# A spectral layer and two MLPs on one core: the first half's instructions issued from one written list of 1092 pieces

## The chip, the cores and the metric

One Trainium2 chip, one of its cores. The metric is the device time of one execution, in microseconds (us). The engines are PE (TensorE, matrix products; PEld is its weight load), DVE (VectorE), ACT (ScalarE), POOL (GpSimd) and SP (SyncE, which issues the DMAs here). Each engine runs its own instructions strictly in their order and waits at the head of its queue until what that instruction needs is there.

## The reference

```python
X = np.fft.fft(x, axis=1)            # x: 2 x 3008 x 256
X = np.fft.fft(X, axis=2)
x = X.real.reshape(6016, 256)
h = x @ w_in                         # 256 x 2048
x = np.maximum(h, 0.0) ** 2 @ w_out  # 2048 x 256
h = x @ w2_in
return h * (1.0 / (1.0 + np.exp(-1.702 * h))) @ w2_out
```

The weights come as float64 words, which the kernel itself turns into a high and a low float32r part.

## The kernel before

The work has three stages on one core.

**Folds and transforms.** The input is loaded in six pieces (`load_x`, L117; three per batch). A *fold* (`fold`, L275) adds and subtracts mirrored positions on DVE and POOL, and then multiplies with a table of cosines and sines on PE (L317). `even_k` (L373) and `odd_k` (L405) finish the transform for the four blocks of frequencies of a batch (L361 on PE) and split each block into a high and a low part (`split_eo`, L364). There are eight blocks, four per batch.

**The first MLP** is 128 *steps*, one for each pair of a block and one of 16 groups of 128 hidden features (`turns`, L445). A step has a *front* (`front1`, L451): six matmuls into two PSUM banks (tile `psa`; the pool has two places). Then DVE makes `p` and two `h` from these banks (L805, L807, L808), ACT takes relu and square (L814, L815; for the steps in `SV`, DVE does both in one instruction, L812), ACT casts to the high part `gh` (L817), and the low part `gl = h - gh` is subtracted on POOL or, for the ten steps in `VSTEPS`, on DVE (both print as L78). Four steps later (`LAG`) the *back* (`back`, L467) adds 12 matmuls (L477) into two PSUM tiles `psb`. Below, F8 is the front of step 8 and B8 its back. `h` and `gh` rotate through five places, `gl` through four.

The weights of both MLPs are widened in the background of the steps: `narrow` (L164) turns the words into float32 by six instructions on ACT and DVE (L171 to L187), `widen` (L194) makes the two parts. Eight such groups of the first MLP are loaded and widened while its steps already run, and so are four of the second MLP's.

**The second MLP** (L872, L856 and what lies between) is written by hand in an explicit order, `manual_schedule`, and begins where the first MLP's last front ends.

**What sets the order before.** `start` (L517) emits the first three folds and the first transforms; then the loop over the steps emits one front, one back, the DVE and ACT work of the step, and calls `background` (L567), which takes a few pieces from the running jobs by the rates and due times of the table `PLAN` (L32). From step 18 (`THROTTLE`) a job's pieces are held behind the step's own work. The tile framework's scheduler then orders the emitted instructions of each engine.

## Time and profile before

| | |
|---|---|
| three runs | 974.51, 975.67 (median), 976.25 us |
| the profiled execution | 974.99 us, span 973.2 us |
| mean granted TensorE clock | 0.998 |
| DMA | 53.58 MB, mean 55 GB/s |

The span is the time from the first to the last instruction. A busy PE in the profile is not PE at its peak: the ends of pipelined matmuls are modelled, so two matmuls that follow each other at 0.17 us each show 0.33 us. Prices below are therefore taken from start to start.

### The profile page before, as it was taken

What the parts mean: (1) busy time and instruction counts of PE and PEld (TensorE: products, weight loads), DVE (VectorE), ACT (ScalarE), POOL (GpSimd) and SP (SyncE); (2) the same over time, 40 slices, a digit from 0 to 9 for tenths busy, and PEclk for the clock granted to TensorE, in tenths of its full rate; (3) what the DMA queues carried; (4) which work ended last, traced back from release to release, by engine and by line L of the source; (5) the groups of instructions that cost most, each with busy time, mean ns of one, the idle gap of its engine ahead of it and who ended that gap; (6) DMA issues with size and microseconds to landing.
All of it is one profiled execution on the core that took longest, in us unless ns stands there. A gap on an engine that the chain in (4) does not pass through costs nothing.

```text
span 973.2 us, 12586 instructions
## 1 busy us (share of the span) xinstructions
PE 954.7 (98%) x4872; PEld 852.9 (88%) x4872; DVE 699.6 (72%) x870; ACT 599.6 (62%) x700; POOL 329.3 (34%) x203
## 2 busy tenths in 40 slices
...
GB/s 303 208 148 64 76 133 93 137 35 57 9 67 44 33 1 47 67 6 33 51 112 44 1 87 0 1 65 22 1 44 43 1 1 82 1 1 10 34 1 39
DMA packets 21899, 53.58 MB, mean 55 GB/s; under 512 B 3280, under 2 KB 15184, under 8 KB 19152
## 3 DMA queue, kind: packets, MB, share of 16 engines
...
q8 instruction: 38, 0.62, 0.3%
q14 instruction: 21, 0.17, 0.1%
...
## 4 chain that ended last, share of the span: by engine, by line
PE 76%; DVE 5%; ACT 3%; issue 1%; DVEq 0%; ACTq 0%
PE psb L872 26%; PE psc L856 23%; PE psb L477 17%; PE psa L462 3%; PE psa L464 3%; PE psa L463 3%; PE psa L361 1%; ACT h L815 1%; ACT h L814 1%; ACT gh L817 1%; DVE h L807 1%; DVE p L805 0%; DVE h L808 0%; PE psa L317 0%; DVE ue L185 0%
## 5 line engine op out<-in xcount | busy, mean ns | idle before, releaser
L78 POOL TENSOR_TENSOR gl<-h,gh 128x752 fp32r<-128x752 f32 (+1 forms) x118 | 223.2, 1897 | 152.5 <-ACT gh L817 108.6
L477 PE MATMUL psb<-gh,w 128*128 128x376 f32 (+1 forms) x1024 | 237.3, 335 | 0.2 <-ACT h L814 0.2
L477 PEld LDWEIGHTS psb<-gh,w 128*128 128x128 f32 x1024 | 182.6, 188 | 0.7 <-ACT h L814 0.4
L872 PE MATMUL psb<-gh,w 128*128 128x512 f32 (+1 forms) x576 | 163.7, 386 | 0.0
L936 DVE TENSOR_TENSOR g<-u,psc 128x1024 f32<-128x1024 f32 (+1 forms) x48 | 57.6, 1201 | 115.4 <-PE psc L856 115.4
L814 ACT ACTIVATE h<-h 128x752 f32<-128x752 f32 (+1 forms) x114 | 94.8, 833 | 58.1 <-DVE h L808 48.0
L477 PE MATMUL psb<-gl,w 128*128 128x376 f32 (+1 forms) x512 | 130.1, 335 | 0.0
L938 ACT ACTIVATE g<-g 128x1536 f32<-128x1536 f32 (+1 forms) x48 | 70.4, 1467 | 95.1 <-DVE g L936 95.1
L872 PEld LDWEIGHTS psb<-gh,w 128*128 128x128 f32 x576 | 108.1, 188 | 20.6
L817 ACT CAST gh<-h 128x752 fp32r<-128x752 f32 (+1 forms) x128 | 105.1, 822 | 31.8 <-DVE h L812 28.5
L78 DVE TENSOR_TENSOR gl<-g,gh 128x2048 fp32r<-128x2048 f32 (+1 forms) x48 | 109.5, 2282 | 1.2 <-ACT gh L913 1.2
L638 POOL TENSOR_TENSOR ue<-raw 128x512 f32<-128x512 f32 (+1 forms) x10 | 21.5, 2165 | 255.0 <-DMA raw<-ydram 173.6
L805 DVE SCALAR_TENSOR_TENSOR p<-n,w1n_t,psa 128x376 f32<-128x376 f32 (+1 forms) x128 | 76.5, 600 | 43.3 <-PE psa L464 43.1
L815 ACT ACTIVATE h<-h 128x752 f32<-128x752 f32 (+1 forms) x114 | 95.2, 836 | 3.1
L462 PE MATMUL psa<-eo,w 128*128 128x376 f32 (+1 forms) x256 | 88.1, 345 | 5.0 <-DVE h L808 2.7
L477 PEld LDWEIGHTS psb<-gl,w 128*128 128x128 f32 x512 | 92.6, 188 | 0.0
L913 ACT CAST gh<-g 128x2048 fp32r<-128x2048 f32 (+1 forms) x48 | 90.3, 1881 | 0.1
L872 PE MATMUL psb<-gl,w 128*128 128x512 f32 (+1 forms) x288 | 87.7, 386 | 0.0
L463 PE MATMUL psa<-eo,w 128*128 128x376 f32 (+1 forms) x256 | 85.8, 335 | 0.0
L464 PE MATMUL psa<-eo,w 128*128 128x376 f32 (+1 forms) x256 | 85.6, 334 | 0.0
L807 DVE TENSOR_TENSOR h<-p,psa 128x376 f32<-128x376 f32 (+1 forms) x128 | 69.7, 545 | 13.9 <-POOL gl L78 1.0
L935 ACT ACTIVATE g<-psc 128x512 f32<-128x512 f32 (+1 forms) x48 | 28.3, 590 | 76.0 <-PE psc L856 76.0
...
## 6 DMA issues: line engine op xcount, KB each, us to landing
...
xt<-in_x SPq DMA_DIRECT2D x5, 1024.0 KB, 7.0
...
raw<-in_w1i SPq DMA_DIRECT2D x4, 1024.0 KB, 4.9
raw<-in_w1o SPq DMA_DIRECT2D x4, 1024.0 KB, 5.8
raw<-in_w2i SPq DMA_DIRECT2D x4, 1024.0 KB, 4.9
raw<-in_w2o SPq DMA_DIRECT2D x4, 1024.0 KB, 4.9
```

Source lines behind the costliest of these rows:

```text
L78: eng.tensor_tensor(out=o, in0=a, in1=f32(b), op=ALU.subtract)
L462: T.matmul(o, lhsT=w[:, 0, fs], rhs=t[:, par, 0, 0:wd], start=True, stop=False)
L463: T.matmul(o, lhsT=w[:, 0, fs], rhs=t[:, par, 1, 0:wd], start=False, stop=False)
L464: T.matmul(o, lhsT=w[:, 1, fs], rhs=t[:, par, 0, 0:wd], start=False, stop=True)
L477: T.matmul(acc[j][ec][:, s, 0:wd], lhsT=w[:, hl, e0:e0 + P], rhs=(gh, gl)[gi][:, s, 0:wd], start=(first and hl == 0 and gi == 0), stop=(la ...
L807: V.tensor_tensor(out=h[:, 0, 0:wd], in0=p[:, 0:wd], in1=ps[:, 1, 0:wd], op=ALU.add)
L814: A.activation(out=hv, in_=hv, func=AF.Relu)
L815: A.activation(out=hv, in_=hv, func=AF.Square)
L817: last_a = A.copy(gh[:, :, 0:wd], hv)
L856: T.matmul(bank, lhsT=w[:, hl, slot * P:(slot + 1) * P], rhs=x[:, yl, 0:wd], start=(first and hl == 0 and yl == 0), stop=(hl == 1), skip_g ...
L872: T.matmul(o[:, s, 0:wd], lhsT=w[:, hl, e0:e0 + P], rhs=g[:, 2 * i + s, 0:wd], start=(f == 0 and hl == 0 and g is gh), stop=(f == 15 and h ...
L913: A.copy(gh, gs[u - 1])
```

## The change

Everything up to the last step of the first MLP is cut into 1092 named pieces, and a written list `ORDER` says in which order they are issued, under `manual_schedule`. `PLAN`, the rates and the background jobs are gone. The names: `f0D` loads input piece 0, `f0s0`, `f0a0`, `f0p`, `f0m`, `f0u` are its sums and differences, `f0E` and `f0O` its products on PE, `f0e0`, `f0o` the moves out of PSUM; `e00..` and `o0..` belong to the transforms of a batch (`E`, `N` products, `c`, `n` copies, `s`, `m` sums, `h`, `l` the two parts); `i0..` to `u3..` widen the first MLP's input and output weights, `j..` and `v..` the second's (`D` load, `A` `L` `C` `S` `O` `P` the six instructions of `narrow`, `H` and `l` the parts). Of step 8, `F8` is the front, `P8` the three DVE instructions, `R8` relu and square, `H8` the cast, `G8` the low part, `B8` the back.

With it some work changes its engine (`HOME`): 43 of the 128 subtractions `G` are on DVE, where ten were; 22 steps have relu and square on DVE, where 14 had; all subtractions of the first three folds are on DVE, where POOL had half or all of them; of the stores' copies six go from DVE to ACT and three from ACT to DVE. Some products of the start go to `psb` (`IN_B`). The two banks of a `psa` tile are now places of their own, and the turn in which `h`, `p` and the banks are taken is written out (`RINGS`). Fold 0 leaves out one sum (`u`) and has PE add instead: 12 products where there were 8, twice. Of the products with zeros that only keep PE at work (`keep_busy`) 26 stay of 48. From the second MLP on nothing changes.

```diff
-PLAN = {
-    "out0": (0, 12, 3), "even01": (0, 1, 4), "odd0": (1, 1, 48), "conv": (3, 1.2, 36),
-    "x3": (14, 1, 20), "x4": (33, 1, 34), "fold3": (31, 1.5, 40), "fold4": (38, 1.5, 46), "fold5": (45, 1.5, 52),
-    "cst": (30, 5, 45), "even10": (53, 1, 56), "even11": (52, 1, 58),
-    "cst3": (66, 4, 67), "odd1": (79, 1, 88), "w2a": (58, 1, 84), "w2b": (88, 1, 112), "y0": (111, 1, 128),
-}
...
-WARM = {0: 36, 2: 4, "first": 3, "second": 5}
-THROTTLE = 18
...
-VSTEPS = {44, 45, 50, 69, 71, 79, 82, 99, 101, 109}
...
-SV = {49, 51, 58, 68, 70, 72, 78, 80, 88, 89, 98, 100, 102, 108}
...
+WARM = {0: 24, 2: 2}
+HOME = {**dict.fromkeys("""j0L X3.1 X7.1 X15.1 X79.1 X95.1 X111.1""".split(), "A"), **dict.fromkeys("""f3s0 i1l i0l u0l i3l G44 G45 G50 G69 G71 G79 G101 G109 e01l o02l i2M i3M e10l e11l o13l y0 ybl0 ybl1""".split(), "G"), **dict.fromkeys("""f4s0 f5s0 u1l u3l G82 G99 u0L v0L v1L e00c e00n G5 u1L G8 G9 R12 G16 G17 X15.0 G22 G23 G24 G25 G28 G35 G37 G40 G47 G48 R54 e10n R56 G54 R58 G55 e11c R60 R62 G61 G63 j01 G64 G65 X63.0 G70 G74 G75 G77 G78 R80 R81 v0l o1c0 R83 o1c1 G81 R85 o12n G86 G87 G91 G92 R96 R97 R98 o13n G96 X95.0 R103 R104 R111 G112 R115 v1l R116 G114 G115 R117 R120 R121 G119 R123 G122 G123 G125 G126 G127""".split(), "V")}
+IN_B = ('f0O', 'f1O', 'f2O', 'e00N', 'e01E', 'e01N', 'o0E0', 'o0E1')
...
+f0D f0a1 f0a0 nyD dfD f0s0 f0p ny f0s1 f0m f1D nD f1s0 f1a0 f1p nA f0E f1m f2D i0D i0A f1u f2s0 f2a0 f0O f2m f1O f2p f2u
+f1E nL f0e0 i0C seD i0L f0e1 f2E nC f1o i0O c00D u0D ma f1e1 f0o f1e0 i0S i0P f2O f2e0 f2o i0M i0N nO c03D se c01D i1D
...
+F4 o0E1 R2 P3 G0
+F5 i1C P4 R3 H2 o0s0 o0c1 G1 i1S u0l u1A o0s1 i1O G2 o02h B0 P5 R4
+F6 H3 B1 P6
...
+F10 P9 i1H B4 P10
+F11 G7 B5 R9 H8 B6 P11 H9 u1S G8 R10 i1l R11 u1O
+F12
...
+    "h": "0123401234012340341203243102431430214302140231402314023140231024310243410234102341023410232341023410"
+          "234102341240312403124031241203412034120341203234102341",
...
+    def of(ring, n):
+
+        return dict(tag=f"{ring}.{next(places[ring])}", bufs=1) if ring in places else dict(tag=ring, bufs=n)
...
+        def bank(self, i):
+            if i not in self.tiles:
+                self.tiles[i] = psa.tile([P, 512], F32, **of(f"a{i}", 2), name="psa")
+            return self.tiles[i]
...
+    ops = {}
+
+    def op(name):
+        def keep(f):
+            ops[name] = f
+            return f
+        return keep
+
+    def on(name, usual):
+        return {"V": V, "A": A, "G": G}[HOME.get(name, usual)]
...
+        @op(name + "L")
+        def _():
+            lw, hw, u, uu, eu = words()
+            if on(name + "L", "A") is A:
+                A.activation(out=eu, in_=lw, func=AF.Copy, scale=2.0 ** -29)
+            else:
+                V.tensor_scalar(out=eu, in0=lw, scalar1=2.0 ** -29, scalar2=None, op0=ALU.mult)
...
-            yield lambda: (
-                *(e.tensor_tensor(out=t[:, 1, i], in0=xt[:, 0, i], in1=xt[:, 1, i], op=ALU.subtract)
-                  for e, i in (((G, slice(0, 4)), (V, slice(4, 8))) if q in (1, 2) else ((G, a),))),
-                V.tensor_tensor(out=t[:, 0, a], in0=xt[:, 0, a], in1=xt[:, 1, a], op=ALU.add),
...
+            @op(f"f{q}s{k}")
+            def _(k=k, a=a):
+                on(f"f{q}s{k}", "V").tensor_tensor(out=whole()[:, 1, a], in0=xq[q][:, 0, a], in1=xq[q][:, 1, a], op=ALU.subtract)
...
+                even = [[(gv[:, :, i], j, s * i) for i in range(2) for j in range(2)] for s in range(2)]
...
+            ps = held[par] = ps_b() if name in IN_B else ps_a()
...
-        yield from fold(0, fold_nyquist)
-        yield from fold(1)
-        yield from fold(2)
-        first = both(widen(0, 0, 0, wq, winp, tag="w", then=lambda: load_w(0, 0, 1)), small_w())
-        for _ in range(14):
-            yield next(first)
-        yield from both(even_k(0, 0, h_temps), first)
-        load_c(0, 3)
...
-    def background(i):
-        for name, rate, job in plan.pop(i, ()):
-            live.append((name, rate, job()))
-        for entry in list(live):
-            if not run(entry[2], int((i + 1) * entry[1]) - int(i * entry[1])):
...
-            if THROTTLE <= i < n:
-                behind.enter_context(tc.issue_after(last_v.ins))
-                behind.enter_context(tc.issue_after(last_a.ins))
-            background(i)
...
+        @op(f"P{i}")
+        def _(i=i, j=j, f=f, wd=wd, st=st):
+            ps = st["ps"]
+            h = st["h"] = m.tile([P, 2, NP], F32, **of("h", 5), name="h")
+            p = m.tile([P, NP], F32, **of("p", 2), name="p")
+            V.scalar_tensor_tensor(out=p[:, 0:wd], in0=e128[blocks[j]][:, 0:wd], scalar=w1n_t[:, 0, f:f + 1],
+                                   in1=ps[:, 0, 0:wd], op0=ALU.mult, op1=ALU.add)
+            V.tensor_tensor(out=h[:, 0, 0:wd], in0=p[:, 0:wd], in1=ps[:, 1, 0:wd], op=ALU.add)
...
+        @op(f"R{i}")
+        def _(i=i, wd=wd, st=st):
+            hv = st["h"][:, :, 0:wd]
+            if on(f"R{i}", "A") is V:
+                V.scalar_tensor_tensor(out=hv, in0=hv, scalar=0.0, in1=hv, op0=ALU.max, op1=ALU.mult)
+            else:
+                A.activation(out=hv, in_=hv, func=AF.Relu)
+                A.activation(out=hv, in_=hv, func=AF.Square)
...
+        @op(f"G{i}")
+        def _(i=i, j=j, f=f, wd=wd, st=st):
+            gh = st["gh"]
+            gl = mg.tile([P, 2, NP], F32R, **of("gl", 4), name="gl")
+            sub(on(f"G{i}", "G"), gl[:, :, 0:wd], st["h"][:, :, 0:wd], gh[:, :, 0:wd])
+            gst[j, f] = gh, gl
...
+        if i < n - LAG:
+            ops[f"B{i}"] = lambda i=i: back(*steps[i][1:])
...
+    with tc.manual_schedule():
+        for name in ORDER.split():
+            ops.pop(name)()
+    assert not ops, list(ops)
```

On ACT, the start, before (L328 moves the folds' products out of PSUM with a bias, L171 and L182 are the first instructions of `narrow`, L339 moves `zs`):

```order
L328 ACT_TABLE_LOAD
L328 ACTIVATE zc<-psa,nyq 128x65 x8
L339 COPY zs<-psb 128x512
L328 ACTIVATE zc<-psa,nyq 128x65 x8
L171 ACTIVATE ue<-raw 128x1024
L159 CAST sel_t<-sel_raw 128x128
L161 COPY mask<-sel_raw 128x1
L339 COPY zs<-psb 128x512
```

and now (L321 and L327 are those of `narrow`, L598 and L308 the moves out of PSUM):

```order
L321 ACT_TABLE_LOAD
L321 ACTIVATE w1n_t<-w1n_raw 128x16
L321 ACTIVATE ue<-raw 128x1024
L327 ACTIVATE w1n_t<-w1n_raw 128x16
L598 ACTIVATE zc<-psa,nyq 128x65 x4
L327 ACTIVATE ue<-raw 128x1024
L598 ACTIVATE zc<-psa,nyq 128x65 x4
L308 COPY zs<-psb 128x512
L495 COPY mask<-sel_raw 128x1
```

Two instructions that need weight words from DRAM now stand ahead of the first move out of PSUM, which stood first.

On DVE, steps 8 to 12, before (L604 is a store's copy):

```order
L805 SCALAR_TENSOR_TENSOR p<-n,w1n_t,psa 128x376
L807 TENSOR_TENSOR h<-p,psa 128x376
L808 TENSOR_TENSOR h<-p,psa 128x376
L604 COPY o<-psb 128x2x376
L805 SCALAR_TENSOR_TENSOR p<-n,w1n_t,psa 128x376 x2
L807 TENSOR_TENSOR h<-p,psa 128x376
```

and now (L1040 to L1043 are `p` and `h`, L214 the low part, L1049 relu and square, L339, L345, L351 and L334 `narrow`):

```order
L1043 TENSOR_TENSOR h<-p,psa 128x376
L339 TENSOR_SCALAR ue<-ue 128x1024
L214 TENSOR_TENSOR gl<-h,gh 128x2x376
L345 SCALAR_TENSOR_TENSOR ue<-raw,ue 128x1024
L214 TENSOR_TENSOR gl<-h,gh 128x2x376
L351 ISA ue<-ue 128x2048
L1040 SCALAR_TENSOR_TENSOR p<-n,w1n_t,psa 128x376
L1042 TENSOR_TENSOR h<-p,psa 128x376
```

Between two steps' `p` and `h`, which read PSUM, DVE now runs low parts and weight passes, which read and write SBUF alone.

On PE, the first fronts, before (L462 to L464 front, L361 transforms, L271 products with zeros):

```order
L463 MATMUL psa<-eo,w 128x378
L464 MATMUL psa<-eo,w 128x378
L271 MATMUL psb<-still 128x128 x5
L361 MATMUL psa<-cst,zc 128x188 x2
L361 MATMUL psa<-cst,zc 128x376 x8
L462 MATMUL psa<-eo,w 128x378
```

and now (L750 to L752 front, L626 transforms):

```order
L626 MATMUL psb<-cst,zc 128x188 x4
L626 MATMUL psb<-cst,zs 128x188 x4
L750 MATMUL psa<-eo,w 128x378
L751 MATMUL psa<-eo,w 128x378
L752 MATMUL psa<-eo,w 128x378
```

The second block's transform stands ahead of the first front as a whole, in `psb`; before, it lay in pieces between the fronts and shared `psa` with them.

## Rows read from the trace of the kernel before

**Rows 1.** The page: busy time, share of the span and instructions of each engine

```profile
PE 954.7 (98%) x4872; PEld 852.9 (88%) x4872; DVE 699.6 (72%) x870; ACT 599.6 (62%) x700; POOL 329.3 (34%) x203
```

**Rows 2.** Windows: stretch, length, busy us (instructions) of PE, PEld, DVE, ACT, POOL; clock, DMA

```profile
0.00:69.47 69.47, 62.94 (x370) 51.82 (x371) 59.78 (x85) 40.22 (x66) 32.47 (x29) 0.98 0.62 231
69.47:147.64 78.17, 76.12 (x433) 74.23 (x433) 62.03 (x95) 66.48 (x84) 55.72 (x30) 1.00 0.26 91
147.64:474.42 326.78, 323.32 (x1863) 313.71 (x1863) 265.16 (x393) 239.88 (x304) 195.83 (x116) 1.00 0.14 46
```

**Rows 3.** Windows of line L477 alone (backs, 12 matmuls each)

```profile
0.00:69.47 69.47, 9.15 (x48) 8.38 (x48) 0.98 0.62 231
```

**Rows 4.** Waits of PE: who for whom, us in total, times, longest

```profile
PE psa L361 <- DVE ue L420: 2.9, 2, 2.5
PE psa L462 <- DVE h L808: 2.7, 7, 1.0
```

**Rows 5.** Timeline of PE, start: start, us, line, operation, count, idle before

```profile
1.03 10.58 PE L271 MATMUL psa<-still 128*128 128x128 f32 x72 [1.03 <-DVE still L266]
11.46 1.95 PE L317 MATMUL psa<-dft,xt 128*128 128x130 f32 x16
...
24.34 1.33 PE L361 MATMUL psa<-cst,zc 128*128 128x189 f32 x8
...
39.09 5.34 PE L361 MATMUL psa<-cst,zc 128*128 128x188 f32 x20
...
50.33 4.55 PE L361 MATMUL psa<-cst,zs 128*128 128x376 f32 x12 [2.54 <-DVE ue L420]
```

**Rows 6.** Timeline of PE in the steps: two backs begin, the next front begins

```profile
279.64 0.51 PE L477 MATMUL psb<-gh,w 128*128 128x378 f32 x2
...
283.80 0.33 PE L462 MATMUL psa<-eo,w 128*128 128x378 f32 x1
```

**Rows 7.** Timeline of DVE: its first wait, and a step with a weight pass

```profile
6.75 0.69 DVE L283 TENSOR_TENSOR t<-xt 128x512 f32<-128x512 f32 x1 [1.43 <-DMA xt<-in_x]
...
63.33 0.59 DVE L805 SCALAR_TENSOR_TENSOR p<-n,w1n_t,psa 128x376 f32<-128x376 f32 x1
63.84 1.21 DVE L185 SCALAR_TENSOR_TENSOR ue<-raw,ue 128x1024 uint32<-128x1024 uint32 x1
64.98 0.53 DVE L807 TENSOR_TENSOR h<-p,psa 128x376 f32<-128x376 f32 x1
65.43 0.53 DVE L808 TENSOR_TENSOR h<-p,psa 128x376 f32<-128x376 f32 x1
```

**Rows 8.** Timeline of ACT: its first moves out of PSUM

```profile
13.89 1.76 ACT L328 ACTIVATE zc<-psa,nyq 128x65 f32<-128x65 f32 x8
```

**Rows 9.** DMA issued at 4.16 us: KB, us to landing

```profile
raw<-in_w1i SPq DMA_DIRECT2D x1, 1024.0 KB, 11.1
```

**Rows 10.** DVE groups by form, 69.5 to 147.6 us: busy us, mean ns

```profile
L175 DVE TENSOR_SCALAR ue<-ue 128x1024 f32<-128x1024 f32 x3 | 5.4, 1789 | 0.6 <-ACT ue L171 0.6
L187 DVE CUSTOM_DVE_ANT_0 ue<-ue 128x2048 uint16<-128x2048 uint16 x3 | 5.0, 1675 | 0.0
L185 DVE SCALAR_TENSOR_TENSOR ue<-raw,ue 128x1024 uint32<-128x1024 uint32 x3 | 4.9, 1640 | 0.0
...
L176 DVE TENSOR_SCALAR ue<-ue 128x1024 uint32<-128x1024 uint32 x3 | 2.1, 684 | 0.0
L208 DVE SCALAR_TENSOR_TENSOR ue<-ue,mask 128x512 f32<-128x512 f32 x2 | 2.0, 982 | 0.0
...
L78 DVE TENSOR_TENSOR w<-ue,w 128x1024 fp32r<-128x1024 f32 x1 | 1.9, 1861 | 0.0
```

**Rows 11.** DVE, the ten low parts: duration ns min/median/max, first and last start

```profile
L78 DVE TENSOR_TENSOR gl<-h,gh x10: 932/1364/1758, 197.6 to 421.5; 128x752 fp32r<-128x752 f32 x7, 128x756 fp32r<-128x756 f32 x3
```

**Rows 12.** Timeline of DVE and of POOL near 123 us

```profile
123.22 2.61 DVE L187 CUSTOM_DVE_ANT_0 ue<-ue 128x2048 uint16<-128x2048 uint16 x1
...
122.89 1.84 POOL L78 TENSOR_TENSOR gl<-h,gh 128x752 fp32r<-128x752 f32 x1 [2.41 <-DVE ue L176]
```

More of the change, by code (lines that the diff above doesn't have):

```diff
@@ new lines, in keep_busy, with _ @@
+            T.matmul(o, lhsT=still, rhs=still, start=True, stop=True, skip_group_check=True)
+    consts = {}
+    @op("dfD")
+    def _():
+        consts["dft"] = zp.tile([P, 2, 258], F32, tag="dft", name="dft")
+        nc.sync.dma_start(consts["dft"], dftd.rearrange("p (s l) -> p s l", s=2))
+    @op("nyD")
+    def _():
+        nc.sync.dma_start(x128_t, x128)
+    @op("nD")
+    def _():
+        nc.sync.dma_start(w1n_raw, w1n.bitcast(U32))
+    @op("seD")
+    def _():
+        consts["sel"] = m.tile([P, NP], F32, **of("p", 2), name="sel_raw")
+        nc.sync.dma_start(consts["sel"][:, 0:P + 1], sel)
@@ L492, in run @@
         return True
-    def both(*gens):
-        gens = list(gens)
-        while gens:
-            for g in list(gens):
-                item = next(g, None)
-                if item is None:
-                    gens.remove(g)
-                else:
-                    yield item
-    def chain(*gens):
-        for g in gens:
-            yield from g
     def h_temps():
-        return [m.tile([P, 2, NP], F32, tag="h", name="ht", bufs=5) for _ in range(2)]
+        return [m.tile([P, 2, NP], F32, **of("h", 5), name="ht") for _ in range(2)]
     def temps_of(pool):
@@ new lines, in spectral_two_mlps_kernel, with _ @@
+    for g in range(2):
+        widen_in(f"j{g}", g, lambda: temp(cv2), [(lambda g=g: (w2a, w2b)[g])] * 2)
+        widen(f"v{g}", 1, 1, g, lambda: temp(cv2), lambda g=g: (w2a, w2b)[g])
+    ops["jlD"] = lambda: load_w(1, *order[4], slot=1)
+    ops["yD"] = lambda: load_y(0)
+    @op("=x")
+    def _():
+        nonlocal cv2, w2a
+        xp.release()
+        cv2 = tc.alloc_tile_pool(name="cv2", bufs=1, side="left", reuse_waits="tile")
+        w2a = tc.alloc_tile_pool(name="w2a", bufs=3, side="left", reuse_waits="tile")
@@ L582, in spectral_two_mlps_kernel, with _, store @@
+    @op("=c")
+    def _():
+        nonlocal w2b
+        cp.release()
+        zp.release()
+        w2b = tc.alloc_tile_pool(name="w2b", bufs=3, side="left", reuse_waits="tile")
+    cv2 = w2a = w2b = None
     leaving = {}
-    def ahead(j):
+    def store(k):
+        j, f = steps[k][1:3]
         wd = WID[blocks[j][1]]
-        leaving[j] = [m.tile([P, 2, NP], F32, tag="h", name="o", bufs=5) for _ in range(2)]
-        for ec, o in enumerate(leaving[j]):
-            nc.sync.dma_start(o[:, :, 0:wd], ydram[j][:, ec, :, 0:wd])
@@ L607, in spectral_two_mlps_kernel, with _ @@
-    pend = None
+        last = [i for i in range(k) if steps[i][4] and steps[i][1] == j]
+        y = once(lambda: dram.tile([P, 2, 2, NP], F32, tag=f"y{j}_{f}", name="ydram"))
+        if last:
+            @op(f"Y{k}")
+            def _():
+                leaving[j] = [m.tile([P, 2, NP], F32, **of("h", 5), name="o") for _ in range(2)]
+                for ec, o in enumerate(leaving[j]):
+                    nc.sync.dma_start(o[:, :, 0:wd], ydram[j][:, ec, :, 0:wd])
+        for ec in range(2):
+            @op(f"X{k}.{ec}")
+            def _(ec=ec):
+                ap = acc[j][ec][:, :, 0:wd]
+                o = (leaving[j][ec] if last else m.tile([P, 2, NP], F32, **of("h", 5), name="o"))[:, :, 0:wd]
+                if last:
+                    V.tensor_tensor(out=o, in0=o, in1=ap, op=ALU.add)
+                else:
+                    copy(on(f"X{k}.{ec}", "AV"[ec]), o, ap)
+                nc.sync.dma_start(y()[:, ec, :, 0:wd], o)
+                if ec:
+                    ydram[j] = y()
@@ L720, in w_tile, with passes @@
         return pool.tile([P, 2, 1024], dtype, tag="w", name="w2")
+    def passes(raw, ue, key):
+        narrow("late", lambda: raw, lambda: ue)
+        return [ops.pop("late" + x) for x in ("ALCSOP" if key in RA else "ACSLOP")]
     def w2_late():
```

820 lines of the change are left out of this document (470 added, 350 removed).

## Prediction

> **What bounds the kernel now.** First the page's line of busy times: PE is busy 98% of the span, the next engine, DVE, 72% [rows 1]. So only PE's idle time can be won, and a busy PE still hides small gaps. I then cut the span where the change ends: front F8 starts at 69.47 us, F32 at 147.64, the second MLP's first product at 474.42 [rows 2]; behind that nothing changes, so I carry a gain there unchanged to the end. The three stretches have 6.5, 2.1 and 3.5 us in which PE is not busy. But by 69.47 PE has done only eight fronts and four backs (48 matmuls, 12 each [rows 3]): in the first stretch it is kept waiting, and fills that time with products with zeros and with matmuls that run late. The list of PE's waits names DVE first: 2.9 us before the odd transform, 2.7 before fronts [rows 4]. The timeline shows the largest: 2.54 us of idle time at 50.33, behind which 12 matmuls take 4.55 us where 20 took 5.34 [rows 5], with the granted clock below full in this stretch (0.98 in the mean, 1.00 later [rows 2]). DVE was busy 59.8 of the first 69.47 us; there it is DVE that sets the pace.
>
> **Start to F8.** Prices go from start to start. A sum over 512 columns on DVE is 0.69 us, a weight pass with two inputs 1.14, the three instructions `p`, `h`, `h` of a step 0.51 + 2 x 0.46 = 1.43 [rows 7]. A back on PE is 2.08 (4.16 for two), a front half of it, 1.04 [rows 6]; 16 products of a fold are 1.95, a first transform, 24 instructions, 3 x 1.33 = 4.0, half an odd one 16/20 of 5.34 = 4.3 [rows 5].
>
> I walk the new list. DVE's first fold waits for the second half of the input, 6.75 us [rows 7]; three differences and sums and one further sum stand ahead of PE's first product, not six with POOL in between: 6.75 + 4 x 0.69 = 9.5, where PE now starts at 11.46 [rows 5]. Of the products with zeros 48 instructions stay of 72 that took 10.4 us; they end near 8, so PE idles a microsecond. Should the clock fall there, it costs at most the 1.3 us lost at 50 us (4.55 against 12/16 of 4.3), and I take nothing. PE then does 24 instructions where 16 were, twice, about 2.0 more. ACT's new head of queue matters: it waits for weight words that land at 4.16 + 11.1 = 15.3 [rows 9], makes a pass of about DVE's 1.2 and moves the first fold out of PSUM from about 16.6, where it did so at 13.89 [rows 8]. Behind it lie 24 small moves of 0.22 [rows 8], one more pass and three larger moves; the last that the first transform needs ends near 24.5. Queued behind them on PE is only that transform: 23.9 to 26.6 (before from 24.34), so this wait is hidden by DVE's folds, which end at about 20.
>
> From there the whole second transform runs on PE while DVE, ACT and POOL finish the first block's parts: F0 at 30.6. From F2 on a front waits for DVE's `p` and `h` two fronts back, 1.43 each with 3.5 us of weight passes between the first three: F3 at 39.7 behind half an odd transform, F4 at 40.9, the other half until 46.6, then F5, B0, F6, B1, F7, B2 one behind the other, F8 at 56.3. From below: PE's own work there is 13.7 (folds) + 8.0 + 8.6 (transforms) + 8.3 (8 fronts) + 6.2 (3 backs) + 0.3 = 45.1, on 9.5: 54.6. On top comes the slowing of the next paragraph: nine weight passes lie beside POOL's work here, at 0.37 each 3.3, of which I let two thirds through, 2.2: **F8 at 58.5**. There three backs are done and not four, so the old kernel's time for equal work is 69.47 - 2.08 = 67.4. Gain 8.9 (ends: 54.6 gives 12.8; each of the nine slowed by 1.1 gives 66.2 and 1.2).
>
> **F8 to F32.** What was put off is paid here. Instructions of DVE with SBUF operands alone are slowed while POOL works: in this stretch 15 of them (L175, L187, L185, three each, L176 three, L208 two, one L78) took 21.3 us [rows 10] where they take 13.9 undisturbed (L175, L176, L208 0.68 and the others 1.21, as the quickest rows show [rows 7, 10]), 0.49 more each, with POOL busy 55.7 of 78.2 us, 71% [rows 2]. Those with a PSUM operand do not show it (0.53 and 0.59 [rows 7]). The list puts 36 such instructions here, ten of them low parts (0.93 at the least, median 1.36 [rows 11]). DVE's work: 24 x 1.43 = 34.3, the 36 at 0.68 to 1.21 undisturbed 30.2, three stores' halves 1.9: 66.4. POOL keeps 15 low parts and six larger pieces, about 41 us or 54%, so I take 0.49 x 54/71 = 0.37 for each: 13.4, together **79.8**. PE has 24 x 1.04 + 23 x 2.08 = 72.8; ACT, busy 66.5 before [rows 2], has about as much. With two places in `psa` PE waits for DVE, so DVE's sum counts. Before, the equal work (a back less) took 78.17 - 2.08 = 76.1: 3.7 lost. Ends: PE's 72.8 (3.3 won) and 36 x 1.1, the mean that L175 lost, (66.4 + 39.6 = 106, 30 lost). The ten low parts of before lost 0.43 in the median [rows 11], so I stay with the lower value.
>
> **F32 to the second MLP.** PE's idle time was 326.78 - 323.32 = 3.5; DVE's new sum is about 240 undisturbed for 103 such instructions, 278 with 0.37 each, against 327 of PE, so it bounds only short pieces. I take 2 won (ends 3.5 won, 3 lost). SP issues the same DMAs with the same sizes in another order. Whether one comes late I can bound only by the 11.1 us of the crowded start [rows 9]; later the DMA engines are busy 0.26 and 0.14 of the time [rows 2], and I take nothing.
>
> **Edits at nothing.** The relus moved to DVE free ACT, which is not late; the stores' copies likewise. PE's 22 fewer products with zeros lay in waits. The rings' written turns move no work.
>
> **Sum.** 8.9 - 3.7 + 2 = 7.2. The profiled execution took 974.99, 0.7 below the median of 975.67: 974.99 - 7.2 = **967.8**.
>
> **A rule against it.** Near 123 us a weight pass on DVE took 2.61 us: POOL had begun 0.33 earlier and ended at 124.73, and 1.1 later DVE was done [rows 12]. So it stood still, and did not share; each moved low part can do so. By SBUF — State Buffer (Who interferes with whom) of the Trainium skill, an instruction of DVE with two SBUF inputs and one of POOL take a shared pair of ports by an exclusive lock, and the later one blocks until the other is done. The trace at 123 us agrees; the page has no price for a mix. Taken at its word, with arrivals at random, it gives rival 2's 974.7 in place of 967.8.
>
> **Rivals.**
> 1. *DVE never binds.* POOL's pieces fall where DVE is on PSUM, and F8 to F32 goes at PE's pace, 74 with small gaps: 8.9 + 2.1 + 3 = 14, 961.0. For: DVE was idle 16 us there [rows 2]. Against: ACT needs some 67 of the 74 too. Chance 0.22.
> 2. *Blind arrival.* Whoever comes meets a POOL instruction with chance 0.54 and waits half of its 1.84 [rows 12], 0.50 each: nine of them 4.5, F8 at 60.8, gain 6.6; 36 of them 18, DVE 84.4, 8.3 lost; then 2 won: 974.7, no change. For: 123 us. Against: 0.71 x 0.92 = 0.65 would have been seen, where 0.49 was. Chance 0.10.
> 3. *DVE becomes the bound (slower).* The low parts now stand on DVE right between POOL's own, whose turn they await: mean loss as of the L78 and L175 of [rows 10], (0.65 + 1.11)/2 = 0.88; 36 x 0.88 = 31.7, F8 to F32 takes 98.1, 22.0 lost, 8.9 won, nothing after: 988.1. It decides from a loss of (8.9 + 2 + 9.7)/36 = 0.57 on. For: L78 and L175. Against: L176, which lost nothing, and less work on POOL. Chance 0.12.
>
> That the list is not what the engines run is excluded: the compiled order follows it on each.
>
> **How the numbers follow.** Forecast 0.54, with its own range 963 to 972; the rivals 0.22, 0.10, 0.12; 0.02 for what I have not seen. The range 959 to 976 leaves out rival 3 and a little on the other side. About 0.2% (2 us) is what a measurement of this kernel can tell from no change. Faster by more: 0.54 + 0.22 + 0.01 = 0.77. Same: 0.09, rival 2. Slower: 0.12 + 0.02 = 0.14.
>
> **What would show it.** Right: PE's first fold product near 9.5; ACT's first move at 16 to 17; F0 near 30.6, F8 near 58.5 with three backs done; F8 to F32 about 80 with PE waiting for DVE's `h`, F32 near 138; the second MLP's first product near 467, 474.42 - 7.2. Wrong: F8 beyond 64, a mean loss of DVE's SBUF instructions beyond 0.57, or a new wait of more than 2 us for a DMA or for ACT.

## The result, and the profile after

The change takes **960.93 us** (median of 4 runs, 960.16 to 962.26), the kernel before 975.86 beside it: ratio 0.9851, 95% interval 0.9834 to 0.9868, 14.9 us less. The direction is the forecast's and the time lies inside the stated range of 959 to 976, but it is 6.9 us beyond the value of 967.8 and outside the forecast's own, narrower range of 963 to 972; it is the time of rival 1. The profiled execution took 960.73 us, its span is 959.0 (before 973.2).

The page's line of busy times, which answers to [rows 1]:

```profile
PE 946.6 (99%) x4844; PEld 849.3 (89%) x4844; DVE 701.3 (73%) x919; ACT 581.2 (61%) x688; POOL 261.8 (27%) x161
```

The windows of the change, cut at F8, at F32 and at the second MLP's first product, answer to [rows 2], with the columns as there and the rest of the span as a fourth stretch:

```profile
0.00:58.26 58.26, 54.06 (x331) 46.31 (x331) 47.47 (x82) 36.50 (x68) 21.54 (x19) 0.97 0.52 192
58.26:133.38 75.12, 73.96 (x421) 72.02 (x421) 69.64 (x107) 69.50 (x87) 39.37 (x20) 1.00 0.32 108
133.38:461.85 328.47, 326.87 (x1888) 317.71 (x1887) 271.27 (x432) 224.91 (x290) 157.38 (x94) 1.00 0.17 57
461.85:959.00 497.15, 491.70 (x2209) 413.30 (x2208) 312.92 (x301) 250.32 (x245) 43.54 (x28) 1.00 0.09 31
```

A back is 2.08 us [rows 6]. At F8 three backs are done (before: four), at F32 26 (before: 28), at the end of the third row 124 (before: 124). With the backs that differ taken off or added, the old stretches for equal work are 67.4, 76.1, 330.9 and 498.8 (973.2 - 474.42). So the change won 9.1 + 1.0 + 2.5 + 1.6 = 14.2 us of span.

What PE still waits for, over the whole span, answers to [rows 4] (us in total, times, longest):

```profile
PE psa L750 <- DVE h L1043: 2.3, 7, 0.4
PE psa L577 <- DVE xt L533: 1.8, 1, 1.8
...
PE psb L765 <- DVE ue L714: 1.0, 1, 1.0
PE psa L750 <- DVE p L1040: 0.6, 1, 0.6
```

The two waits of the transforms that stood in [rows 4] and [rows 5] are gone. The start on PE, beside [rows 5]:

```profile
10.17 4.46 PE L577 MATMUL psa<-dft,xt 128*128 128x130 f32 x24 [1.84 <-DVE xt L533]
...
24.88 1.33 PE L626 MATMUL psa<-cst,zc 128*128 128x189 f32 x8
...
31.55 0.44 PE L750 MATMUL psa<-eo,w 128*128 128x378 f32 x1
...
50.54 0.59 PE L765 MATMUL psb<-gh,w 128*128 128x378 f32 x2 [1.04 <-DVE ue L714]
```

The groups of DVE from F8 to F32 that answer to [rows 10] and [rows 11] (busy us, mean ns): the low parts moved to DVE take 0.93 to 0.94 there, with no loss.

```profile
L351 DVE CUSTOM_DVE_ANT_0 ue<-ue 128x2048 uint16<-128x2048 uint16 x4 | 6.4, 1603 | 0.0
L214 DVE TENSOR_TENSOR gl<-h,gh 128x752 fp32r<-128x752 f32 x7 | 6.4, 934 | 0.0
L345 DVE SCALAR_TENSOR_TENSOR ue<-raw,ue 128x1024 uint32<-128x1024 uint32 x4 | 5.1, 1276 | 0.0
...
L334 DVE TENSOR_SCALAR ue<-ue 128x1024 f32<-128x1024 f32 x4 | 4.4, 1103 | 0.0
```

Against the undisturbed prices (1.21, 0.93, 1.21, 0.68) the stretch's 32 instructions with SBUF operands alone lost 4.3 us: 1.6 in L351, 1.7 in L334, 0.3 in L345, 0.7 in one relu with square. That is 0.13 each. The forecast had 0.37 for each of 36. A *loss* here and below is the time that an instruction took beyond its undisturbed price.

### The profile page after: what moved, and what is told of

Read it like the earlier page. It is cut to its first block, busy times and chain, and to the rows that moved or that the text cites. A ratio compares the mean times of both kernels' runs of the same rounds, so it can differ in the third digit from the quotient of the medians.

```text
span 959.0 us, 12390 instructions
## 1 busy us (share of the span) xinstructions
PE 946.6 (99%) x4844; PEld 849.3 (89%) x4844; DVE 701.3 (73%) x919; ACT 581.2 (61%) x688; POOL 261.8 (27%) x161
## 4 chain that ended last, share of the span: by engine, by line
PE 63%; DVE 1%; issue 0%; ACT 0%; DVEq 0%
PE psb L1112 27%; PE psc L1096 24%; PE psb L765 9%; PE psa L750 1%; PE psa L752 1%; PE psa L751 1%; DVE gl L214 0%; DVE h L1042 0%; DVE h L1043 0%; DVE g L1176 0%; DVE w L214 0%; DVE p L1040 0%; DVE h L1049 0%; DVE o L1202 0%; ACT o L1200 0%
## 5 line engine op out<-in xcount | busy, mean ns | idle before, releaser
L765 PE MATMUL psb<-gh,w 128*128 128x376 f32 (+1 forms) x1024 | 234.2, 335 | 1.1 <-DVE ue L714 1.0
L214 POOL TENSOR_TENSOR gl<-h,gh 128x752 fp32r<-128x752 f32 (+1 forms) x85 | 165.1, 1947 | 169.3 <-PE psb L765 65.6
L1057 ACT CAST gh<-h 128x752 fp32r<-128x752 f32 (+1 forms) x128 | 103.0, 818 | 53.4 <-PE psb L765 51.1
L214 DVE TENSOR_TENSOR gl<-g,gh 128x2048 fp32r<-128x2048 f32 (+1 forms) x48 | 109.9, 2290 | 1.2 <-ACT gh L1153 1.2
L1051 ACT ACTIVATE h<-h 128x752 f32<-128x752 f32 (+1 forms) x106 | 88.1, 831 | 25.3 <-DVE h L1043 23.4
L881 POOL TENSOR_TENSOR ue<-raw 128x512 f32<-128x512 f32 (+1 forms) x11 | 23.7, 2169 | 254.1 <-DMA raw<-ydram 247.8
L1040 DVE SCALAR_TENSOR_TENSOR p<-n,w1n_t,psa 128x376 f32<-128x376 f32 (+1 forms) x128 | 76.9, 601 | 19.9 <-PE psa L752 19.6
L750 PE MATMUL psa<-eo,w 128*128 128x376 f32 (+1 forms) x256 | 88.0, 344 | 3.0 <-DVE h L1043 2.3
L1052 ACT ACTIVATE h<-h 128x752 f32<-128x752 f32 (+1 forms) x106 | 88.7, 836 | 3.4
L1042 DVE TENSOR_TENSOR h<-p,psa 128x376 f32<-128x376 f32 (+1 forms) x128 | 70.0, 547 | 25.2 <-POOL gl L214 6.4
L752 PE MATMUL psa<-eo,w 128*128 128x376 f32 (+1 forms) x256 | 85.5, 334 | 0.0
```

What stands on the lines that cost most here:

```text
L214: eng.tensor_tensor(out=o, in0=a, in1=f32(b), op=ALU.subtract)
L750: T.matmul(o, lhsT=w[:, 0, fs], rhs=t[:, par, 0, 0:wd], start=True, stop=False)
L752: T.matmul(o, lhsT=w[:, 1, fs], rhs=t[:, par, 0, 0:wd], start=False, stop=True)
L765: T.matmul(acc[j][ec][:, s, 0:wd], lhsT=w[:, hl, e0:e0 + P], rhs=(gh, gl)[gi][:, s, 0:wd], start=(first and hl == 0 and gi == 0), stop=(la ...
L1040: V.scalar_tensor_tensor(out=p[:, 0:wd], in0=e128[blocks[j]][:, 0:wd], scalar=w1n_t[:, 0, f:f + 1], in1=ps[:, 0, 0:wd], op0=ALU.mult, op1= ...
L1051: A.activation(out=hv, in_=hv, func=AF.Relu)
```

## The experiments

Places are given as F8, F32, F48 and "MLP2", the second MLP's first product. The change has them at 58.26, 133.38, 189.16 and 461.85. A run is compared with the 960.93 of the change or with the kernel before that ran beside it (974 to 977); F0 is the first front.

**1. The new order with the old engines.** `HOME` is the change's, but each step's low part and relu go where the kernel before had them (the edit written short):

```diff
+HOME = {n: e for n, e in HOME.items() if not re.match(r"[GR]\d+$", n)}
+HOME.update({f"G{x}": "V" for x in VSTEPS}, **{f"R{x}": "V" for x in SV})
```

> The change with the low parts and the relus of the first MLP's steps on the engines they had before (10 low parts on DVE instead of 43, 14 relus instead of 22, and other ones); order, turns and start as in the change. Theory A, the written order carries the gain: F8 to F32 is bounded by PE with either choice; POOL gets 9 low parts back in that stretch (9 x 1.84 = 16.6 us, from 52% to 74%), DVE gives 9 x 0.94 = 8.5 us away; F8 stays at 58 to 59, F32 within 1 us of 133.4, the whole within 2 us of the change, 960 to 963. Theory B, the engine choice carries it: POOL at 74% brings back the loss of 0.49 us for each of the 23 instructions of DVE with SBUF operands alone that stay in the stretch and makes the low parts late; PE waits for them before the backs, F32 at 138 or later, the whole 966 or more.

Measured: 970.03 (969.34 to 970.99). F8 at 56.69 (the input came 1.5 us earlier than in the change; from F0 to F8 both take 26.7), F32 at 137.08 (80.4 for the stretch), F48 at 191.16, MLP2 at 471.75. POOL is busy 60.92 of the 80.39 us, 76%, and DVE's 22 instructions with SBUF operands alone lose 11.7 us, 0.53 each. The timeline of DVE and of POOL shows how (start, us):

```profile
67.11 1.80 DVE L333 TENSOR_SCALAR ue<-ue 128x1024 uint32<-128x1024 uint32 x1
68.83 3.39 DVE L339 SCALAR_TENSOR_TENSOR ue<-raw,ue 128x1024 uint32<-128x1024 uint32 x1
72.25 2.72 DVE L345 CUSTOM_DVE_ANT_0 ue<-ue 128x2048 uint16<-128x2048 uint16 x1
74.89 0.59 DVE L1034 SCALAR_TENSOR_TENSOR p<-n,w1n_t,psa 128x376 f32<-128x376 f32 x1
...
66.53 1.82 POOL L208 TENSOR_TENSOR gl<-h,gh 128x752 fp32r<-128x752 f32 x1 [2.75 <-ACT gh L1051]
68.31 2.82 POOL L208 TENSOR_TENSOR w<-ue,w 128x1024 fp32r<-128x1024 f32 x1
71.09 5.53 POOL L208 TENSOR_TENSOR gl<-h,gh 128x752 fp32r<-128x752 f32 x2
```

While both have such work queued they take turns (each with SBUF operands alone), and each pass of DVE first stands through a piece of POOL's: 7.9 us for passes of 0.68, 1.21 and 1.21. Theory B holds for the time; PE's waits, however, are for DVE's `h` (4.3 us in 12 waits) and not for low parts. The start, as theory A said, needs none of these moves.

**2. The old order with the new engines.** The kernel before, with the change's engines for the low parts and the relus of the steps and nothing else of it; the framework's scheduler still orders the instructions.

```diff
-VSTEPS = {44, 45, 50, 69, 71, 79, 82, 99, 101, 109}
-SV = {49, 51, 58, 68, 70, 72, 78, 80, 88, 89, 98, 100, 102, 108}
+VSTEPS = [5, 8, 9, 16, 17, 22, 23, 24, 25, 28, 35, 37, 40, 47, 48, 54, 55, 61, 63, 64, 65, ...]
+SV = [12, 54, 56, 58, 60, 62, 80, 81, 83, 85, 96, 97, 98, 103, 104, 111, 115, 116, 117, ...]
```

> The kernel before, with the change's choice of engines for the low parts (43 on DVE) and the relus (22 on DVE), in the old order. Theory A, the written order carries the gain: here the moved low parts meet POOL where they fall, DVE loses 0.37 us or more for each of some 25 instructions in F8 to F32, and PE's waits for h grow: 976 to 982, no gain over the kernel before. Theory B, the engine choice carries it: POOL's share in the stretch falls from 71% to about 50%, DVE's loss falls below 0.2 us each, and the kernel gains 2 us or more: 974 or less.

Measured: 986.84 (984.63 to 988.96), ratio 1.0115, 1.0095 to 1.0136: slower than before by 11.0. Windows from F8 to F32 and from there to MLP2:

```profile
70.51:152.78 82.27, 77.77 (x434) 75.65 (x433) 70.88 (x105) 66.26 (x82) 37.39 (x21) 0.98 0.25 86
152.78:484.73 331.95, 326.06 (x1863) 314.72 (x1863) 282.10 (x420) 227.30 (x289) 157.22 (x94) 0.99 0.14 45
```

POOL is down to 45%, and DVE's 26 instructions lose 7.5 us, 0.29 each. Theory A has the direction, but the time is beyond its 976 to 982 and the loss is below its 0.37. The loss alone does not explain it: in total it is about what the kernel before lost there (7.2), while DVE is busy 70.9 us instead of 62.0, and PE's waits for `p` and `h` grow from 3.9 to 8.8 us over the span. The order, with the edits of the start, gives -5.8 us, the steps' engines alone +11.0, both together -14.9: neither half is worth what it seems alone.

**3. More products with zeros.**

```diff
-WARM = {0: 24, 2: 2}
+WARM = {0: 30, 2: 2}
```

> The change with 30 products with zeros ahead of the first fold instead of 24 (12 instructions more, 0.15 us each: 1.8 us, which is PE's idle time before its first fold). Theory A, the idle time lets the granted clock fall to 0.5 from 11.4 to 14.8 us and PE's late folds set the path: the clock stays at 1.0, the folds end some 1.3 us earlier, F0 at 30.3, the whole 959.6. Theory B, ACT sets the path there (its first move out of PSUM waits for weight words until 15.95 and a pass of 1.2): the clock stays up, but F0 stays at 31.5 and the time within 0.4 us of the change's 960.9.

Measured: 959.10 (958.87 to 959.33), theory A's number and not its reason. Windows from 10.2 to 15 us, of this kernel and then of the change (the granted clock is the third number from the end):

```profile
10.20:15.00 4.80, 4.56 (x41) 4.54 (x41) 4.63 (x11) 0.22 (x1) 0.00 (x0) 1.00 1.01 422
```

```profile
10.20:15.00 4.80, 4.80 (x28) 4.80 (x29) 4.60 (x11) 0.22 (x1) 0.00 (x0) 0.64 1.00 418
```

The clock no longer fell (in the change PE stood at its lower level, 1.2 GHz, for some of these us, behind 1.84 us without work), but F0 stands 21.3 us behind PE's first fold product in both (31.79 - 10.46 and 31.55 - 10.17): DVE's sums come no sooner, and PE waits 1.0 for one instead. The time came from F32 to F48: 54.08 us, in the change 55.78. DVE and the DMA issues of the change near F32, and then the same DMA in this run (KB, us to landing):

```profile
132.69 0.55 DVE L1042 TENSOR_TENSOR h<-p,psa 128x378 f32<-128x378 f32 x1 [0.56 <-DMA ydram<-o]
ydram<-o SPq DMA_DIRECT2D x1, 376.0 KB, 4.2
```

```profile
ydram<-o SPq DMA_DIRECT2D x1, 376.0 KB, 2.8
```

In the change this `h` waits until an output copy has been stored from the place that it takes, and the low part G28 and the weight pass u3P behind it on DVE come later, u3P after a low part of POOL's has begun (experiment 9). Here the store landed sooner, `h` did not wait, and u3P began 0.13 us ahead of POOL (136.71 against 136.84) and took 1.22. Why the store was quicker here no run shows, so the gain is not credited to the six added products. Experiments 9 to 12 follow the collision.

**4. The transforms back in the fronts' place.**

```diff
-IN_B = ('f0O', 'f1O', 'f2O', 'e00N', 'e01E', 'e01N', 'o0E0', 'o0E1')
+IN_B = ('f0O', 'f1O', 'f2O')
```

The written turns of the two banks (`a0`, `a1`) are gone with it, since they no longer fit; experiment 7 drops all turns and leaves F0 to F8 at 26.7, so what follows is the place's.

> The change with the transforms' outputs in psa again (in turn with the fronts' places, as before) where the change puts five of them into psb. Theory A, the place carries much of the start's gain: the second transform occupies places that the first fronts need, and a front waits for DVE to empty them; F8 comes 2 to 5 us later, 60.5 to 63.5, the whole 963 to 966. Theory B, the order of the start on DVE and ACT carries it and a place is free in time: F8 at 58 to 59, the whole within 0.5 us of 960.9.

Measured: 966.03 (964.46 to 966.94); F0 at 30.83, F8 at 61.24. From F0 to F8 it takes 30.4 us where the change takes 26.7. The timeline of PE shows the waits in between, 4.4 us with three more, where the change has 1.3:

```profile
37.71 0.44 PE L742 MATMUL psa<-eo,w 128*128 128x378 f32 x1 [1.02 <-DVE h L1035]
...
47.86 3.63 PE L618 MATMUL psa<-cst,zs 128*128 128x376 f32 x14 [1.44 <-DVE h L1035]
```

Theory A, with F8 inside its range and the whole at its upper end: of the start's 9.1 us, 3.7 hang on the place of these outputs.

**5. Part of the first folds back on POOL** (the edit written short).

```diff
+HOME.update(dict.fromkeys(("f0s0", "f0s1", "f1s0", "f2s0"), "G"))
```

> The change with four sums or differences of the first folds on POOL again (1.77 us each there, 0.69 on DVE, as before). Theory A, taking POOL out of DVE's way carries part of the start's gain: PE's first fold product comes about 1 us later, DVE's weight passes beside POOL stretch, F0 and F8 come 1 to 3 us later, the whole 962 to 964. Theory B, DVE's time in the folds is not on the path (the weight words and ACT are): F8 within 0.5 us, the whole within 0.7 us of 960.9.

Measured: 961.79 (961.36 to 963.38). F8 comes at 60.49, 2.2 later. 0.3 of that is the input (DVE's first sum begins at 7.79, in the change at 7.49); the other 1.9 come with POOL: DVE waits 2.25 us for POOL's difference, and a sum of 1.22 takes 3.40 beside POOL, part of which is hidden. F32 is at 133.96, only 0.6 later: 1.6 us come back on the way, since the clamp i3C takes 0.69 here and not 2.36 (experiment 10). Theory A for F8; of the whole 0.9 is left.

**6. ACT's waiting operations behind its first moves.**

```diff
-... f1p nA f0E f1m f2D i0D i0A f1u ...
-f1E nL f0e0 i0C seD i0L f0e1 ...
+... f1p f0E f1m f2D i0D f1u ...
+f1E f0e0 seD f0e1 nA i0A nL i0L i0C ...
```

> The change with ACT's four weight operations, the first of which waits 4.7 us for weight words at the head of ACT's queue, put behind its first two moves out of PSUM. Theory A, DVE and PE's folds set the path to F0 (the first transform started right behind the last fold product): nothing won, F0 within 0.4 us, the whole 960.5 to 962. Theory B, the moves' late start (17.1 us) sets it: F0 2 us earlier, the whole 959 or less.

Measured: 960.58 (959.64 to 961.08); F0 again 21.3 us behind the first fold product. Theory A: DVE and PE's folds set F0, and the wait at the head of ACT's queue costs nothing.

**7. No written turns.**

```diff
-RINGS = {"a0": ..., "a1": ..., "gh": ..., "gl": ..., "h": ..., "p": ...}
+RINGS = {}
```

> The change without the written turns in the rings (the places of psa, p, h, gh and gl rotate). Theory A, the turns matter, since in the searched order a place that was given out later is often free sooner: PE waits for a place in psa that DVE has not emptied, 1 to 5 us lost between F8 and the second MLP, the whole 962 to 966. Theory B, the turns only write down what rotation gives nearly everywhere: within 0.7 us of 960.9.

Measured: 956.94 (956.45 to 958.10), 4.0 faster than the change, which neither theory had. F8 to F32 takes 73.92, F32 to F48 54.03 (change: 75.12 and 55.78), the rest is as in the change within 0.6.

**8. The last two fronts late again.**

```diff
-F126 B118 ... F127 B119 ybH0 ... B121 ... B122 ... B123 G126 G127
+B118 ... B119 ybH0 ... B121 ... F126 P126 R126 B122 yal G124 F127 P127 ... B123 G126 G127
```

> The change with its last two fronts put back to where they stood before, F126 ahead of back 122 and F127 ahead of back 123 (in the change all 128 fronts are done five backs before the second MLP's first product, before one back). Theory A, the 1.6 us that the stretch after the second MLP's first product got shorter come from there: ACT's last relus, squares and casts stand again ahead of the second MLP's own first work, PE waits for g there, that stretch goes from 497.1 back to about 498.8 and the whole to 962 to 963. Theory B, they come from elsewhere: the stretch stays at 497.1, the whole within 0.7 us of 960.9.

Measured: 961.53 (959.90 to 962.49), too near to the change to tell by the time. But the stretch from MLP2 on is 497.8 (959.7 - 461.94) and not 497.1, with one wait back in PE's list:

```profile
PE psc L1089 <- DVE g L1169: 1.1, 1, 1.1
```

The kernel before had it too, and the change does not. PE's first rows of the second MLP, before and then in the change:

```profile
481.30 2.60 PE L856 MATMUL psc<-yc,w2i 128*128 128x512 f32 x9
484.22 1.66 PE L856 MATMUL psc<-yb,w2i 128*128 128x512 f32 x6 [0.32 <-ACT g L935]
487.09 1.64 PE L856 MATMUL psc<-ya,w2i 128*128 128x512 f32 x6 [1.21 <-DVE g L936]
```

```profile
468.73 2.24 PE L1096 MATMUL psc<-yc,w2i 128*128 128x512 f32 x9
470.82 1.52 PE L1096 MATMUL psc<-yb,w2i 128*128 128x512 f32 x6
472.29 1.66 PE L1096 MATMUL psc<-ya,w2i 128*128 128x512 f32 x6
```

From the first to the third row it was 5.8 us and is 3.6. The second MLP's code is the same; what is earlier is the first MLP's last front, done five backs ahead instead of one, so that ACT and DVE have no steps left to finish. Putting two fronts back returned 0.6 of the 1.6 us, with that wait; in the other runs with the change's last fronts the stretch lies between 496.6 and 497.5. For the other 1.0 the cause is argued from the rows and shown by no run.

**9. One pass ahead of one low part.** In the change, DVE and POOL near 137 us (the first low part is G28, L351 is the weight pass u3P):

```profile
136.08 0.94 DVE L214 TENSOR_TENSOR gl<-h,gh 128x756 fp32r<-128x756 f32 x1
136.94 2.85 DVE L351 CUSTOM_DVE_ANT_0 ue<-ue 128x2048 uint16<-128x2048 uint16 x1
...
136.62 4.85 POOL L214 TENSOR_TENSOR gl<-h,gh 128x756 fp32r<-128x756 f32 x2 [4.63 <-ACT gh L1057]
```

```diff
-F31 B25 P31 R29 u3O u3C u3S R30 G28
-F32 R31 B26 u3P P32 H29 G29
+F31 B25 P31 R29 u3O u3C u3S u3P R30 G28
+F32 R31 B26 P32 H29 G29
```

> The change with one entry of the list moved: the narrowing pass u3P (128x2048 words, 1.22 us undisturbed) stands on DVE ahead of the low part G28 instead of behind it. In the change's profile u3P began at 136.94 us, 0.32 us after a low part on POOL, and took 2.85 us; the next front's p came 1.6 us later and PE waited. Theory A, an instruction of DVE that begins a little after POOL's stands until POOL's is done, and one that begins a little before makes POOL stand: u3P begins near 136.1, takes 1.22 us, F32 to F48 shrinks from 55.8 to about 54.1, the whole 959.0 to 959.7. Theory B, the moved pass loses its time anyway (the low part G28 behind it meets POOL instead, or another wait takes its place): within 0.5 us of 960.9.

Measured: 960.40 (960.16 to 960.86), F32 to F48 55.69. The same two engines:

```profile
136.10 1.23 DVE L345 CUSTOM_DVE_ANT_0 ue<-ue 128x2048 uint16<-128x2048 uint16 x1
137.24 2.58 DVE L208 TENSOR_TENSOR gl<-h,gh 128x756 fp32r<-128x756 f32 x1
...
136.73 4.77 POOL L208 TENSOR_TENSOR gl<-h,gh 128x756 fp32r<-128x756 f32 x2 [4.63 <-ACT gh L1051]
```

The pass was saved as theory A said, and POOL stood instead; but then it was POOL's turn, and DVE's next instruction, G28, paid the 1.65 us. Theory B. What counts is what stands *behind* the pass.

**10. Only the turn of `h` taken out.**

```diff
 RINGS = {
...
-    "h": "0123401234012340341203243102431430214302140231402314023140231024310243410234102341023410232341023410"
-          "234102341240312403124031241203412034120341203234102341",
```

> The change with the written turn of the ring h alone taken out (h's places rotate; psa, p, gh and gl as written). Rotation of all rings had taken 4.0 us off the change. Theory A, the turn of h carries that (a place given out of turn makes DVE's h, and so a front two later, wait for a low part or a cast that is still to come): 956.5 to 958.5. Theory B, no turn carries it, and the 4 us are the two collisions of DVE and POOL near 107 and 137 us that fell otherwise in that run: 960 to 961.5, unless those collisions fall otherwise here too, which the two places would show.

Measured: **956.63** (955.98 to 957.40), ratio 0.9804, 0.9789 to 0.9819: below the change's interval. F8 to F32 73.82, F32 to F48 54.10. From F8 to step 21's `h` (101.72 in the change) both kernels do the same within 0.05 us. Then, in the change and below in this run, DVE and POOL:

```profile
106.12 0.55 DVE L1042 TENSOR_TENSOR h<-p,psa 128x376 f32<-128x376 f32 x1 [0.20 <-PE psb L765]
106.58 0.54 DVE L1043 TENSOR_TENSOR h<-p,psa 128x376 f32<-128x376 f32 x1
107.04 2.36 DVE L334 TENSOR_SCALAR ue<-ue 128x1024 f32<-128x1024 f32 x1
...
105.25 3.59 POOL L214 TENSOR_TENSOR gl<-h,gh 128x752 fp32r<-128x752 f32 x2 [0.93 <-ACT gh L1057]
```

```profile
105.39 0.55 DVE L1035 TENSOR_TENSOR h<-p,psa 128x376 f32<-128x376 f32 x1
105.85 0.54 DVE L1036 TENSOR_TENSOR h<-p,psa 128x376 f32<-128x376 f32 x1
106.31 0.78 DVE L327 TENSOR_SCALAR ue<-ue 128x1024 f32<-128x1024 f32 x1
...
104.73 4.04 POOL L207 TENSOR_TENSOR gl<-h,gh 128x752 fp32r<-128x752 f32 x2 [1.02 <-ACT gh L1050]
...
134.60 1.22 DVE L344 CUSTOM_DVE_ANT_0 ue<-ue 128x2048 uint16<-128x2048 uint16 x1
...
134.69 2.83 POOL L207 TENSOR_TENSOR gl<-h,gh 128x756 fp32r<-128x756 f32 x1 [4.65 <-ACT gh L1050]
```

By `ORDER` and `RINGS` the written turn gives step 22's `h` (106.12) the place of an output copy of step 15, and ahead of it DVE stood 0.20 us; in this run it is 0.09. The profile names a back there, but the same 0.20 stands where it names DVE's own `p`:

```profile
65.11 0.55 DVE L1042 TENSOR_TENSOR h<-p,psa 128x376 f32<-128x376 f32 x1 [0.20 <-DVE p L1040]
```

So the rows do not show that `h` waited for a back. The trace of the change has two semaphore instructions of DVE ahead of 7 of its 128 L1042, these two among them; DVE stands 0.20 us ahead of five of the seven and longer ahead of the others, and at most 0.09 where there is no such instruction. The difference is 0.11. POOL's low part also begins 0.10 sooner against `p` (105.25 and 105.33; in this run 104.73 and 104.71). Together they bring the clamp i3C (L334, L327) from 0.2 us ahead of POOL's second low part (106.31 against 104.73 + 1.8) to the same moment (107.04 against 105.25 + 1.8), and there it was DVE that stood.

Near 135 us u3P began 0.09 ahead of POOL, and there the next instruction on DVE has a PSUM operand: POOL stood 1.0 us, and PE waited for nothing. This second collision hangs on the same turn: it gives step 31's `h` the place of step 23's second output copy, whose store it waits for in the change (experiment 3). With the written turn and the change's engines this `h` waits 0.35 to 1.30 us in experiments 4, 5, 6, 8 and 9 too, and behind it an instruction of DVE loses 1.6 us each time. It does not wait in 3, nor in any run where the places of `h` rotate (7, 10, 11, 12).

Both theories are right in part: the turn is the cause, and the two collisions are how.

**11. Four edits together**: those of 3, 6, 7 and 9.

> The change with four edits together: rings that rotate, 30 products with zeros instead of 24 ahead of the first fold, ACT's four weight operations behind its first two moves, u3P ahead of G28. If their effects were independent, 960.9 - 4.0 - 1.8 - 0.3 - 1.6 = 953.2. Theory A, the first two and the last won the same microseconds (the collision near 137 us): 956 to 957.5. Theory B, each adds its own: 953 to 955.

Measured: 959.03 (957.78 to 959.52): neither. F8 to F32 is 73.95 as in experiment 7, but F32 to F48 is 55.77 again: with the swap of experiment 9 on board, G28 takes 2.58 us at 135.57, a collision that rotation alone does not have (experiment 7). The edits are not worth a sum, since each decides anew who comes first.

**12. A delay put in.** Experiment 10, with part of the clamp i3C done twice:

```diff
+            if name == "i3":
+                V.tensor_scalar(out=u[:, 0:640], in0=u[:, 0:640], scalar1=LEAST, scalar2=TOP, op0=ALU.max, op1=ALU.min)
             V.tensor_scalar(out=u, in0=u, scalar1=LEAST, scalar2=TOP, op0=ALU.max, op1=ALU.min)
```

> The kernel of the run with h's written turn taken out (956.6), with one small instruction more on DVE: the clamp i3C is done a first time on 640 of its 1024 columns (about 0.4 us) right ahead of itself. In that run i3C began at 106.31 us, 0.24 us before POOL's second low part, and took 0.78; in the change it came 0.11 us later against the rest of the list, right behind the start of that low part, and took 2.36. Theory A, 0.1 to 0.4 us on DVE there decide the collision, and this is how the written turn cost its 4 us: i3C takes 2 us or more again, F16 to F32 goes from 49.0 back to about 50.3, the collision near 137 us comes back with it (F32 to F48 from 54.1 to about 55.8), the whole 958.5 to 961. Theory B, the written turn costs through its own waits and the collision is only beside it: 956.5 to 957.2, F32 to F48 stays at 54.1.

Measured: 959.10 (958.92 to 959.55), 2.5 more than experiment 10 for one instruction of 0.59 us:

```profile
106.34 0.59 DVE L328 TENSOR_SCALAR ue<-ue 128x640 f32<-128x640 f32 x1
106.96 2.19 DVE L329 TENSOR_SCALAR ue<-ue 128x1024 f32<-128x1024 f32 x1
```

F8 to F32 went from 73.82 to 75.85: 0.6 of that is the added instruction, 1.4 the clamp. F32 to F48 stayed at 54.11: u3P began 0.09 us ahead of POOL again. Theory A for the first collision, not for the second: that one does not follow from the first but from the store of experiment 3, and here `h` rotates.

## Why the prediction was right, and where a term was not

- **As a whole**: the direction and the stated range were right. The stated range held because it took in rival 1, with a chance of 0.22; the forecast's own range, 963 to 972, was missed, since DVE did not become the bound from F8 to F32 as it said.
- **Start to F8**: forecast 58.5 with three backs and a gain of 8.9; 58.26 with three and 9.1. PE's first product came at 10.17 (9.5), the input being 0.7 later than in the run of before [rows 7]; ACT's first move at 17.1 (16.6), F0 at 31.55 (30.6), F3 at 40.2 (39.7). That F8 agrees to 0.2 is partly luck: F0 is 1.0 later than forecast, and from F0 to F8 it takes 26.7 where 27.9 were forecast. The start's edits carry the gain: experiment 1 keeps it with the old engines of the steps. Experiment 4 gives 3.7 of it to `psb`, experiment 5 some 1.9 to POOL being out of the folds; no run splits the rest. That ACT's wait is hidden was right (experiment 6), and so was pricing the fallen clock at nothing (experiment 3).
- **F8 to F32**: this is the mis-sized term, "36 x 0.37 = 13.4, together 79.8", 3.7 lost. It took 75.12, 1.0 won. The step that failed is taking the loss in proportion to POOL's share. The proportion of before, 0.49 at 71%, gives 0.52 at experiment 1's 76% (measured 0.53), 0.31 at experiment 2's 45% (0.29), and 0.36 at the change's 52%, where 0.13 was measured. In this stretch it holds in the runs whose order and engines do not belong together, but it is no rule: from F32 on the kernel before lost 0.58 each with POOL at 60%, where the proportion gives 0.41. In the change order and engines fit: of its nine low parts on DVE here, seven run with no instruction of POOL beside them and two begin before POOL's. DVE's sum was 69.6 and not 79.8, and did not bind. (The reading of 0.68 as L208's undisturbed price is 0.06 too low, by its quickest instance of 0.74; that changes 0.49 to 0.48.)
- **F32 to the second MLP**: 2 forecast, 2.5 measured. The loss per instruction was 0.16 here (16.1 us over 103), before 0.58 (39.7 over 69).
- **Edits at nothing**: "The rings' written turns move no work" missed that they decide what an instruction waits for. Without them the kernel is 4.0 us faster, without that of `h` 4.3 (experiments 7 and 10). "I take nothing" for a late DMA missed the store of experiment 3, a wait of 0.56 us that led to a collision of 1.6.
- **After that**: "behind that nothing changes, so I carry a gain there unchanged" missed 1.6 us. The code is the same, but what the engines still had in hand when it begins is not (experiment 8).
- **The sum**: 7.2 forecast, 14.2 of span measured; 4.7 of the difference lies in the second term, 1.6 in the last, 0.5 and 0.2 in the others.
- **The rivals**: rival 1 has the time (961.0) and the reason that DVE does not bind, though its 14 were made up otherwise. Rivals 2 and 3 fell with the loss of 0.13. But rival 3's picture, DVE's work standing between POOL's and awaiting its turn, is what experiment 1 looks like near 70 us. Experiment 2 came out slower, as rival 3 had it, but with a loss of 0.29 and not of 0.57 or more.
- **The rule weighed** (the Trainium skill, SBUF — State Buffer, Who interferes with whom: whoever begins first holds the shared pair of ports for the whole instruction, the other blocks): the traces agree in every collision shown in which one clearly began first, on either side; at 107.04 the two are recorded as beginning together, and DVE stood. With arrivals at random it gave 974.7; the arrivals are not random, and the list decides most of them.
